# First pair's second and third unit two and three blocks sooner in the bias, values parts one a block from block 31; last block's products ahead of the scores

## The chip, the cores and the metric

The kernel runs on one core of a Trainium2 chip. The metric is the device time of one execution in microseconds (us). The core has five engines with an instruction queue each, taken in order: TensorE (PE in the profile; PEld is its weight load), VectorE (DVE), ScalarE (ACT), GpSimd (POOL) and SyncE (SP, which only issues transfers here). They wait for each other through semaphores.

## What is computed

Attention with a learned position bias over 4 batches, 8 heads, 576 positions and 64 columns a head, and then a feed-forward layer with a convolution of width 3 and a gate. Cut from the reference:

```python
rel = (pos[:, None] - pos[None, :])
x = (np.log1p(np.abs(rel)) / np.log1p(np.maximum(pos[:, None], 1.0)))[..., None]
bias = np.maximum(x @ w1 + b1, 0.0) @ w2
scores = scale * np.matmul(q, k.transpose(0, 1, 3, 2)) + bias.transpose(2, 0, 1)[None]
attn = softmax(scores)
x = heads_side_by_side(np.matmul(attn, v))
h = np.maximum(x @ w_in, 0.0)
out = (h * sigmoid(conv(h))) @ w_out
```

## The kernel before

The bias comes first. It depends on the row i and on the distance of i and j alone, and it is computed in 36 blocks of 16 rows (`NBLK`). `bias_hidden(blk)` makes the hidden layer of one block, four tiles `y` of four rows each: three on DVE (line 329) and one on ACT (line 325), in blocks 14, 15, 30 and 31 all four on DVE. `bias_mm(blk)` multiplies them with the second layer's weights on PE (operands `y,pars`) into one of two PSUM pairs, and `bias_out(blk)` copies the sums out on ACT (line 372; one call for two blocks from block 4 to block 31, else one a block) and lets SP store them in DRAM as `bias_d`. Four `y` buffers rotate. The DRAM copy is what turns distances into rows: `load_bias(0, t)` reads the bias tile `bt` of 128 query rows (64 for t = 0) back. SP issues stores and loads in the order of the code, and a load waits at the head of SP's queue for the stores that it reads.

The attention goes by pairs of heads, pair (n) by n = 0 to 15, and each pair by five units t of query rows. A unit is: `scores` of head 0 (PE, `qk`), `reduce` of head 0 (DVE, line 480, which adds `bt`, takes the maximum and writes `sp`), the same for head 1, `expo` of each head (ACT, line 494), transposes (PE, line 111), and copies of the transposed tile to `ptx` or `pty` (one on ACT, line 152, two on DVE, line 155). In the first units all scores go through one PSUM pair, so `scores` of head 1 waits until `reduce` of head 0 has read it. After unit 2 of a pair the products with the values can be made: `pv_parts` gives five parts of two matmuls (PE, `ptx,vt`), and with the fifth part a copy of the sum to `x` on ACT (line 152, 128x320).

Four units of the first pair, (0,0) to (0,3), are woven into the 36 blocks. `starts` holds the block at which each begins, and `unit_steps` is a generator that gives one step a block: scores and reduce of head 0, of head 1, then expo of head 0, of head 1, then the transposes with their copies. In one block the code emits first `bias_hidden` of the next block, then a step of PE, then the block's own products, then `bias_out` of the block before. The value parts wait in `fill`, and the loop takes some from block `starts[-1]` on; the rest is emitted after the loop. The second half of unit (0,3), unit (0,4) and all units of the later pairs follow after the loop, two units of scores ahead of the transposes: unit (1,0), (1,1), (1,2), (0,4), (1,3) and so on. Unit (0,4) needs the bias tile of the last 128 rows, which the blocks up to 35 make (`load_bias(0, 4, (96,))`: rows 0 to 95 in one load for each head, the rest in another).

Of the kernel before, what the change touches and what calls it, by code (L numbers as in the profile page):

```python
# [18 lines left out]
def attention_ffn_kernel(  # L19
# [75 lines left out]
    def use(ins, ap):  # L95
        name, engine = ap.tensor.name, ins.ins.engine
        before = {}
        for k in spans[name]:
            if latest[k] and latest[k][1] != name and latest[k][2] != engine:
                before[latest[k][0].ins.name] = True  # L100
            latest[k] = (ins, name, engine)
        for other in before:
            tc.add_manual_dep(ins.ins, other, mybir.DependencyInfo(
                mybir.DependencyClass.Sync, mybir.DependencyReason.DATA))
        return ins

    def mm(o, *args, **kw):
        return use(nc.tensor.matmul(o, *args, **kw), o)  # L108
# [89 lines left out]
    with tc.manual_schedule():  # L198
# [53 lines left out]
        def load_bias(p, t, cuts=()):  # L252
            queue = nc.sync
            bt = bias_p.tile([P, 2, S], F32, name="bt") if t else bias0_p.tile([P, 1, S], F32, name="bt0")
            for a, e in zip((0,) + cuts, cuts + (P,)):
                for h in range(2):
                    c = (2 * p + h) * BW
                    if t:
                        i0 = TL + (t - 1) * P
                        queue.dma_start(bt[a:e, h], bias_rows[i0 + a:i0 + e, c:c + S])  # L260
                    else:
                        queue.dma_start(bt[TL * h:TL * h + TL, 0, :], bias_rows[0:TL, c:c + S])
            biast[p, t] = bt
# [44 lines left out]
        def reach(blk):  # L308
            i0 = 16 * (blk - blk % 2)
            return S - i0, i0 + 31  # L310


        def relu_from(blk):
            return 4 if blk // 2 % 8 == 7 else 3

        def bias_hidden(blk):
            full = max(reach(blk)[0], reach(blk)[1] + 1)
            ys = []
            for j in range(4):
                ig = 4 * blk + j  # L320
                n = max(S - 4 * ig, 4 * ig + 4) if 4 <= blk < 32 else full
                row = ybuf[blk % 4][:, j] if j < 3 else y3[:, blk % 4]
                y = row[:, 0:n]
                if j >= relu_from(blk):
                    nc.scalar.activation(  # L325
                        y, dist[:, 0:n], AF.Relu, bias=pars[:, 1:2], scale=inv[:, ig:ig + 1]
                    )
                else:
                    nc.vector.tensor_scalar(  # L329
                        y, dist[:, 0:n], inv[:, ig:ig + 1], nb1, op0=ALU.mult, op1=ALU.max  # L330
                    )
                ys.append(row[:, 0:full])
            return ys
# [3 lines left out]
        def bias_mm(blk, ys):  # L337
            n = ys[0].shape[1]
            if n > 512 or blk % 2 == 0:
                bias_ps[blk] = wide()  # L340
            else:
                bias_ps[blk] = bias_ps[blk - 1]
            ps = bias_ps[blk]
            for a in range(0, n, 512):
                for j in range(4):
                    mm(
                        ps[32 * j:32 * j + 32, a // 512 if n > 512 else blk % 2, 0:min(n - a, 512)],
                        w2b,
                        ys[j][:, a:min(n, a + 512)],
                        start=True,  # L350
                        stop=True,
                    )

        def bias_out(blk):
            nf, nr = reach(blk)
            n = max(nf, nr + 1)
            ps = bias_ps.pop(blk)
            st = sts[blk // 2 % 5].rearrange("p (b n) -> p b n", b=2)
            if n > 512:
                o, i = st[:, blk % 2:blk % 2 + 1], ps.rearrange("p (b a) x -> p b (a x)", b=1)  # L360
            else:
                o, i = st, ps
            fwd = nf > nr


            if n > 512 or blk % 2:
                k = relu_from(blk) - 3
                for oo, ii in (
                    (slice(nr, nr + nf), slice(0, nf)) if fwd else (slice(0, nr + 1), slice(nr, None, -1)),
                    (slice(0, nr), slice(nr, 0, -1)) if fwd else (slice(nr + 1, nr + nf), slice(1, nf)),  # L370
                ):
                    use(nc.scalar.activation(  # L372
                        o[:, :, oo], i[:, :, ii], AF.Identity, bias=kv[:, k:k + 1], scale=inv_scale
                    ), ps)
            if blk == NBLK - 2:
                at = 64 + blk * P * BW - nr
                nc.sync.dma_start(
                    bias_d[at:at + P * BW].rearrange("(p c) -> p c", c=BW)[:, 0:nr + nf], st[:, 0, 0:nr + nf]
                )
            if blk % 2 == 0:  # L380
                return
            at = 64 + (blk - 1) * P * BW - nr
            dst = bias_d[at:at + 2 * P * BW].rearrange("(b p c) -> p b c", b=2, c=BW)
            if blk == NBLK - 1:
                nc.sync.dma_start(dst[:, 1, 0:nr + nf], st[:, 1, 0:nr + nf])
                return
            nc.sync.dma_start(dst[:, :, 0:nr + nf], st[:, :, 0:nr + nf])
# [32 lines left out]
        def turned_sp(n, t):  # L420
            spt[n, t] = (sps[1][spt[n, t][1]], None)
# [53 lines left out]
        def reduce(n, t, h):  # L475
            bt = biast[seq[n][0], t]
            i = pair.pop((n, t, h))
            ps = pairs[i]
            done(i)
            use(nc.vector.tensor_tensor_reduce(  # L480
                out=halves(spt[n, t][0][:, h]),
                in0=ps[:, :, 0:HS],
                in1=halves(bt[:, h]),
                op0=ALU.add,
                op1=ALU.min,
                scale=-scale,
                scalar=3.0e38,
                accum_out=nms[n, t][:, h:h + 1],
            ), ps)

        def expo(n, t, h):
            sp, nm = spt[n, t][0], nms[n, t]
            col = 4 * h + t - 1 if t else 8
            exps[n, t, h] = nc.scalar.activation(  # L494
                sp[:, h], sp[:, h], AF.Exp, bias=nm[:, h:h + 1], scale=-1.0,
                accum_out=sms[n][:, col:col + 1],
            )
# [242 lines left out]
        flat = [(n, t) for n in range(1, NSEQ) for t in units]  # L740
# [3 lines left out]
        def heads(t):  # L744
            return (0, 1) if t else (0,)

        fill = deque()

        def unit_steps(n, t):

            for h in heads(t):
                scores(n, t, h)
                reduce(n, t, h)
                yield h < heads(t)[-1]
            for h in heads(t):
                expo(n, t, h)
                if h == heads(t)[-1]:
                    turned_sp(n, t)
                yield h == heads(t)[-1]
            side = None  # L760
            if t:
                side = pairs[2][:, :, HS:HS + TL]
                side_transposes(side, n, t)
            place_all(transposes(n, t), n, t, side)
            del spt[n, t]
            if ends_group(n, t):
                fill.extend(pv_parts(n, t > 2))
            yield None

        hidden = bias_hidden(0)  # L770
# [4 lines left out]
        load_v(1)  # L775
        last = None
        unit, on_pe = None, None
        starts = [13, 21, 29, 34]
        for i in range(NBLK):
            nxt = bias_hidden(i + 1) if i + 1 < NBLK else None  # L780
            if i in starts:
                unit, on_pe = unit_steps(*first[starts.index(i)]), True
            stepped = bool(on_pe)
            if on_pe:
                on_pe = next(unit)
            bias_mm(i, hidden)
            if last:
                bias_out(*last)
            last = (i,)
            hidden = nxt  # L790
            if i == 5 or i > 6 and i % 8 == 6:
                load_bias(0, i // 8)
            if on_pe is False and not stepped:
                on_pe = next(unit)
            for _ in range(max(0, i - starts[-1] + 1)):
                fill.popleft()()
        bias_out(*last)
        load_bias(0, 4, (96,))
        scores(*flat[1], 0)
        reduce(*flat[1], 0)  # L800
        for h in heads(flat[0][1]):
            expo(*flat[0], h)
        turned_sp(*flat[0])
        while fill:
            fill.popleft()()
# [7 lines left out]
        for u, (n, t) in enumerate(flat[:7]):  # L813
# [18 lines left out]
            i = turned_in.pop((n, t))  # L832
# [457 lines left out]
```

## Time and profile before

| | us |
|---|---|
| median of 3 runs | 473.8 (473.74 to 475.83) |
| the profiled execution | 473.89 |
| its span, first to last instruction | 472.1 |
| PE busy | 456.6 (97%) |
| DVE busy | 361.0 (76%) |
| ACT busy | 308.1 (65%) |

The profiled execution is one of those that the median stands for; 1.8 us of it lie outside its span. Busy shares are means over the whole kernel: DVE and ACT carry the bias in the first 60 us, PE the rest. The granted clock of PE was 0.996 of full speed in the mean.

### The profile page before, as it was taken

How to read it: one execution, taken by the hardware profiler on the slowest of the kernel's cores; microseconds unless marked ns; L12 is line 12 of the kernel's file. 1: busy time of each engine (PE TensorE's matmuls, PEld its weight loads, DVE VectorE, ACT ScalarE, POOL GpSimd, SP SyncE). 2: the span in 40 equal slices, each digit the busy share in tenths (PEclk: the TensorE clock that was granted, in tenths of full speed). 3: DMA queues.
4: the chain of work that ended last, by engine and by line, in shares of the span. 5: the costliest groups of instructions: out<-in, count | busy, mean ns of one | idle time of the engine just before them, and what ended most of it. 6: DMA issues, size and time to landing. Idle time of an engine off the chain costs nothing.

```text
span 472.1 us, 10937 instructions
## 1 busy us (share of the span) xinstructions
PE 456.6 (97%) x4095; PEld 342.2 (72%) x4095; DVE 361.0 (76%) x833; ACT 308.1 (65%) x754; POOL 155.6 (33%) x182
## 2 busy tenths in 40 slices
PE   5987899999999999999999999999999999999996
PEld 3333356777787768877786678988888888888886
DVE  6999967899999799988998631991698159936971
ACT  6989876898888898888888622961453136414530
POOL 1000000583777437781775535006002400060000
PEclk9989999999999999999999999999999999999999
DMA  6798748699678987688673310002000200020002
GB/s 155 205 340 308 265 159 183 173 277 235 174 174 198 280 198 185 148 290 204 160 168 96 116 51 1 2 1 89 1 0 1 96 16 0 1 91 0 1 11 100
DMA packets 34536, 60.81 MB, mean 129 GB/s; under 512 B 6300, under 2 KB 15028, under 8 KB 34484
## 3 DMA queue, kind: packets, MB, share of 16 engines
q1 hardware_dynamic: 34100, 59.78, 44.9%
q8 instruction: 32, 0.52, 0.5%
q10 hardware_dynamic: 384, 0.35, 0.2%
q14 instruction: 20, 0.16, 0.1%
HBM read 44.12 MB, written 15.98 MB: 127 GB/s over the span
## 4 chain that ended last, share of the span: by engine, by line
PE 88%; DMA 4%; DVE 3%; ACT 3%; SPq 1%; issue 1%; DVEq 0%
PE pair L108 38%; PE bank L108 38%; PE bank L111 10%; DMA bias_d<-st 2%; DVE y L329 1%; DMA qk<-in_qk_dram 1%; PE pair L111 1%; ACT st L372 1%; DVE sp L480 1%; ACT y L325 1%; DMA pars<-in_par_dram 1%; DMA bt<-bias_d 1%; ACT sp L494 1%; DVE ptx L155 0%; ACT tl L372 0%
## 5 line engine op out<-in xcount | busy, mean ns | idle before, releaser
L494 ACT ACTIVATE sp<-sp,nm 128x576 f32<-128x576 f32 x144 | 110.8, 771 | 2.3 <-DVE nm L480 1.3
L480 DVE CUSTOM_DVE_ANT_0 sp<-pair,bt 128x576 f32<-128x576 f32 x144 | 105.4, 751 | 8.3 <-PE pair L108 4.8
L108 PE MATMUL pair<-xs,wi 128*128 128x512 f32 x384 | 88.6, 390 | 0.0
L108 PE MATMUL bank<-wo,g 128*128 128x512 f32 x384 | 87.7, 389 | 0.0
L108 PEld LDWEIGHTS pair<-xs,wi 128*128 128x128 f32 x384 | 71.8, 188 | 15.7 <-issue 0.9
L108 PEld LDWEIGHTS bank<-wo,g 128*128 128x128 f32 x384 | 72.0, 188 | 14.9
L111 PE MATMUL bank<-identr,sr 64*128 64x64 f32 x1184 | 63.1, 246 | 1.9 <-ACT sp L494 1.7
L111 PEld LDWEIGHTS bank<-identr,sr 64*128 64x128 f32 x1184 | 56.0, 136 | 11.1 <-ACT ptx L152 5.4
L1075 DVE SCALAR_TENSOR_TENSOR cv<-h,cw,cv 128x575 f32<-128x575 f32 x64 | 52.4, 818 | 12.6 <-ACT cv L1070 10.6
L694 ACT ACTIVATE h<-pair 128x512 f32<-128x512 f32 x32 | 19.1, 598 | 60.4 <-PE pair L108 55.4
L329 DVE TENSOR_SCALAR y<-tl,inv,nb 128x576 f32<-128x576 f32 (+33 forms) x112 | 47.6, 508 | 0.0
L108 PE MATMUL bank<-ptx,vt 128*64 128x320 f32 x320 | 47.0, 438 | 0.0
L194 POOL TENSOR_SCALAR xs<-x 128x512 fp32r<-128x512 f32 (+1 forms) x16 | 11.2, 702 | 105.4 <-DVE gt L1095 105.3
L233 POOL TENSOR_SCALAR hi<-qk 128x640 fp32r<-128x640 f32 (+1 forms) x27 | 19.2, 711 | 80.9 <-DMA qk<-in_qk_dram 79.4
L108 PE MATMUL pair<-y,pars 128*32 128x512 f32 (+8 forms) x352 | 42.7, 511 | 1.7 <-DVE y L329 0.7
L108 PE MATMUL pair<-qk 64*128 64x288 f32 (+1 forms) x280 | 41.2, 433 | 2.0 <-DVE nm L480 1.8
L236 POOL TENSOR_TENSOR ql<-qk,hi 128x640 fp32r<-128x640 f32 (+1 forms) x27 | 40.9, 1513 | 2.3
L152 ACT ACTIVATE ptx<-bank 128x256 f32<-128x256 f32 (+1 forms) x92 | 33.5, 398 | 12.1 <-PE bank L111 11.3
L108 PE MATMUL bank<-pty,vt 128*64 128x256 f32 x320 | 38.1, 384 | 0.0
L1081 ACT ACTIVATE cv<-cv 128x576 f32<-128x576 f32 x32 | 21.9, 684 | 21.9 <-DVE cv L1075 21.8
L1082 DVE SCALAR_TENSOR_TENSOR cv<-cv,h 128x576 f32<-128x576 f32 x32 | 24.1, 753 | 14.0 <-ACT cv L1081 14.0
L108 PEld LDWEIGHTS pair<-y,pars 128*32 128x32 f32 x352 | 15.4, 114 | 26.3 <-DVE y L329 10.7
(89 smaller groups left out, 704.2 us busy)
## 6 DMA issues: line engine op xcount, KB each, us to landing
qk<-in_qk_dram SPq DMA_DIRECT2D x32, 320.0 KB
bt<-bias_d SPq DMA_DIRECT2D x30, 288.0 KB
bias_d<-st SPq DMA_DIRECT2D x13, 607.0 KB
qk<-in_qk_dram SPq DMA_DIRECT2D x32, 144.0 KB
rb<-r_d SPq DMA_DIRECT2D x32, 144.0 KB
vt<-in_v_dram SPq DMA_DIRECT2D x16, 256.0 KB
raw_w<-in_moe_w_in_dram SPq DMA_DIRECT2D x16, 256.0 KB
out_dram<-o SPq DMA_DIRECT2D x16, 256.0 KB
```

The costliest lines, as they stand in the source:

```text
L108: return use(nc.tensor.matmul(o, *args, **kw), o)
L111: return use(nc.tensor.transpose(o, *args), o)
L152: return noted(nc.scalar.activation(o, i, AF.Copy), i)
L233: first = nc.gpsimd.tensor_scalar(hi[:, cs], x[:, cs], 1.0, 0.0, op0=ALU.mult, op1=ALU.add)
L236: nc.gpsimd.tensor_sub(lo[:, cs], x[:, cs], hi[:, cs].bitcast(F32))
L329: nc.vector.tensor_scalar(y, dist[:, 0:n], inv[:, ig:ig + 1], nb1, op0=ALU.mult, op1=ALU.max)
L480: use(nc.vector.tensor_tensor_reduce(out=halves(spt[n, t][0][:, h]), in0=ps[:, :, 0:HS], in1=halves(bt[:, h]), op0=ALU.add, op1=ALU.min, s ...
L494: exps[n, t, h] = nc.scalar.activation(sp[:, h], sp[:, h], AF.Exp, bias=nm[:, h:h + 1], scale=-1.0, accum_out=sms[n][:, col:col + 1],)
L694: use(nc.scalar.activation(h[:, 0:NM], ps[:, 0], AF.Relu), ps)
L1075: nc.vector.scalar_tensor_tensor(out=cv[:, o:o + S - 1], in0=h[:, i:i + S - 1], scalar=cw[:, f, kk:kk + 1], in1=cv[:, o:o + S - 1], op0=AL ...
L1081: nc.scalar.activation(cv, cv, AF.Tanh, scale=0.5)
L1082: nc.vector.scalar_tensor_tensor(out=cv, in0=cv, scalar=1.0, in1=h, op0=ALU.add, op1=ALU.mult)
```

## The change

Three things are moved, and no instruction is added or removed. In `starts`, unit (0,1) begins at block 19 where it was 21, and unit (0,2) at block 26 where it was 29. The value parts of unit (0,2)'s group are taken one a block from block 31, where they were taken one in block 34, two in block 35 and two behind the loop. In the last block the products of the bias come before the scores of head 1 of unit (0,3), and behind the loop `expo` of that unit's head 0 is emitted before `bias_out(35)`, not behind the scores and the reduce of unit (1,0).

```diff
-        starts = [13, 21, 29, 34]
+        starts = [13, 19, 26, 34]
         for i in range(NBLK):
             nxt = bias_hidden(i + 1) if i + 1 < NBLK else None
             if i in starts:
                 unit, on_pe = unit_steps(*first[starts.index(i)]), True
             stepped = bool(on_pe)
+            if nxt is None:
+                bias_mm(i, hidden)
             if on_pe:
                 on_pe = next(unit)
-            bias_mm(i, hidden)
+            if nxt:
+                bias_mm(i, hidden)
             if last:
                 bias_out(*last)
...
-            for _ in range(max(0, i - starts[-1] + 1)):
+            if i >= 31 and fill:
                 fill.popleft()()
+        expo(*flat[0], 0)
         bias_out(*last)
         load_bias(0, 4, (96,))
         scores(*flat[1], 0)
         reduce(*flat[1], 0)
-        for h in heads(flat[0][1]):
-            expo(*flat[0], h)
+        expo(*flat[0], 1)
         turned_sp(*flat[0])
```

DVE's queue around blocks 20 to 22 (`y_123` to `y_125` are the tiles of blocks 20 to 22, `sp_60` is what the reduces of unit (0,1) write):

```order
 L329 TENSOR_SCALAR y_123<-tl,inv,nb_133 128x332 [waits PE_49]
-L329 TENSOR_SCALAR y_124<-tl,inv,nb_133 128x340 [waits PE_49]
-L329 TENSOR_SCALAR y_124<-tl,inv,nb_133 128x344 [waits PE_49]
-L329 TENSOR_SCALAR y_124<-tl,inv,nb_133 128x348 [waits PE_49]
-L329 TENSOR_SCALAR y_125<-tl,inv,nb_133 128x356 [waits PE_49]
-L329 TENSOR_SCALAR y_125<-tl,inv,nb_133 128x360 [waits PE_49]
-L329 TENSOR_SCALAR y_125<-tl,inv,nb_133 128x364 [waits PE_49]
 L480 ISA sp_60,nm<-pair,bt 128x576 [waits DMAHW1_49,PE_49]
 L480 ISA nm 128x1
+L329 TENSOR_SCALAR y_124<-tl,inv,nb_133 128x340 [waits DVE_49]
+L329 TENSOR_SCALAR y_124<-tl,inv,nb_133 128x344 [waits DVE_49]
+L329 TENSOR_SCALAR y_124<-tl,inv,nb_133 128x348 [waits DVE_49]
```

The reduce of head 0, which waits for a load of `bt`, stood behind the tiles of block 22 and stands behind those of block 20.

PE's queue of the change from the value part of block 34 on (`y_126` is block 35, `qk_55` unit (0,3), `qk_56` unit (1,0)):

```order
L108 MATMUL bank<-ptx,vt_112 64x320 x2
L108 MATMUL pair<-y_126,pars 32x512 [waits DVE_49,Activation_49]
L108 MATMUL pair<-y_126,pars 32x512 [waits DVE_49] x2
L108 MATMUL pair<-y_128,pars 32x512
L108 MATMUL pair<-y_126,pars 32x64 x3
L108 MATMUL pair<-y_128,pars 32x64
L108 MATMUL pair<-qk_55 128x288 [waits DVE_49]
L108 MATMUL pair<-qk_55 128x288
L108 MATMUL bank<-ptx,vt_112 64x320 [waits DMAHW7_49,Pool_49]
L108 MATMUL bank<-ptx,vt_112 64x320 [waits DMAHW0_49]
L108 MATMUL pair<-qk_56 64x288 [waits DMAHW2_49,DMAHW1_49,DVE_49]
```

Before, the scores of unit (0,3), head 1, stood ahead of block 35's products; the first part stood in block 34, two stood behind block 35's products, and two behind unit (1,0).

ACT's queue at the end of the loop (`st_131` is written by `bias_out(34)` and then by `bias_out(35)`, `sp_59` is unit (0,3), `sp_60` unit (1,0), `x_127` the copy that goes with the fifth value part):

```order
 L372 ACTIVATE st_131<-pair,kv 128x31
-L372 ACTIVATE st_131<-pair,kv 128x576 [waits PE_49]
+L152 ACTIVATE x_127<-bank 128x320 [waits PE_49]
+L494 ACTIVATE sp_59,sm<-sp_59,nm 128x576 [waits DVE_49]
+L372 ACTIVATE st_131<-pair,kv 128x576
 L372 ACTIVATE st_131<-pair,kv 128x31
-L494 ACTIVATE sp_59,sm<-sp_59,nm 128x576 [waits DVE_49] x2
-L152 ACTIVATE x_127<-bank 128x320 [waits PE_49]
+L494 ACTIVATE sp_59,sm<-sp_59,nm 128x576 [waits DVE_49]
 L494 ACTIVATE sp_60,sm<-sp_60,nm 128x576 [waits DVE_49]
```

`bias_out(35)` stood directly behind `bias_out(34)`; now the copy of the fifth part's sum and one exponential stand between the two.

## Rows read from the trace of the kernel before

**Rows 1.** Windows; behind the colon the length, then each engine's busy time.

```profile
60.00:80.00 20.00, 19.66 (x214) 11.71 (x214) 13.60 (x41) 14.83 (x40) 0.00 (x0) 1.00 0.72 189
80.00:472.00 392.00, 388.22 (x3471) 311.01 (x3467) 293.05 (x654) 241.34 (x626) 153.91 (x168) 1.00 0.40 107
```

**Rows 2.** Chain of work that ended last, in order of time: start, us, what.

```profile
22.44 2.95 DMA bt<-bias_d
...
57.23 0.80 DVE ptx L155 x2
...
74.09 0.83 PE bank L111 x16
```

**Rows 3.** DVE timeline, several stretches: start, us, instructions, idle before and its releaser.

```profile
33.65 1.20 DVE L329 TENSOR_SCALAR y<-tl,inv,nb 128x340 f32<-128x340 f32 x3
...
42.73 0.29 DVE L155 COPY ptx<-pair 128x128 f32<-128x128 f32 x1 [0.49 <-PE pair L111]
43.43 0.69 DVE L155 COPY ptx<-bank 128x512 f32<-128x512 f32 x1 [0.41 <-PE bank L111]
...
45.29 0.94 DVE L329 TENSOR_SCALAR y<-tl,inv,nb 128x452 f32<-128x452 f32 x2
...
54.24 1.05 DVE L329 TENSOR_SCALAR y<-tl,inv,nb 128x544 f32<-128x544 f32 x2
...
70.23 0.76 DVE L480 CUSTOM_DVE_ANT_0 sp<-pair,bt 128x576 f32<-128x576 f32 x1
```

**Rows 4.** SP timeline, issues of loads and of the last store.

```profile
32.11 0.81 SPq L260 DMA_DIRECT2D bt<-bias_d  x2
...
42.61 0.81 SPq L260 DMA_DIRECT2D bt<-bias_d  x2
...
63.10 0.33 SPq L385 DMA_DIRECT2D bias_d<-st  x1
...
65.75 0.77 SPq L260 DMA_DIRECT2D bt<-bias_d  x2
```

**Rows 5.** PE timeline, blocks 33 to 35 and after.

```profile
56.47 1.13 PE L108 MATMUL pair<-y,pars 128*32 128x512 f32 x16
57.52 0.76 PE L108 MATMUL pair<-qk 64*128 64x288 f32 x4
58.21 1.18 PE L108 MATMUL pair<-y,pars 128*32 128x512 f32 x16
59.32 0.76 PE L108 MATMUL bank<-ptx,vt 128*64 128x320 f32 x4
...
60.91 1.18 PE L108 MATMUL pair<-y,pars 128*32 128x512 f32 x16
62.02 1.30 PE L108 MATMUL bank<-ptx,vt 128*64 128x320 f32 x8
63.24 0.72 PE L108 MATMUL pair<-qk 64*64 64x288 f32 x8
63.89 1.30 PE L108 MATMUL bank<-ptx,vt 128*64 128x320 f32 x8
```

**Rows 6.** ACT timeline behind the last block.

```profile
62.15 0.92 ACT L372 ACTIVATE st<-pair,kv 128x576 f32<-128x576 f32 x2 [1.78 <-PE pair L108]
62.96 0.77 ACT L494 ACTIVATE sp<-sp,nm 128x576 f32<-128x576 f32 x1
...
65.26 0.44 ACT L152 ACTIVATE x<-bank 128x320 f32<-128x320 f32 x1 [0.68 <-PE bank L108]
65.59 0.77 ACT L494 ACTIVATE sp<-sp,nm 128x576 f32<-128x576 f32 x1
```

**Rows 7.** Windows: length, busy PE, PEld, DVE, ACT, POOL; then PE's granted clock.

```profile
25.20:26.90 1.70, 0.36 (x2) 0.00 (x0) 1.34 (x4) 1.49 (x3) 0.00 (x0) 1.00 1.05 409
...
28.60:32.20 3.60, 3.60 (x24) 1.63 (x24) 3.55 (x11) 2.91 (x6) 0.00 (x0) 0.53 1.02 392
...
40.50:42.20 1.70, 0.25 (x2) 0.00 (x0) 1.70 (x5) 1.70 (x4) 0.00 (x0) 1.00 0.56 220
```

## The prediction

> **What bounds the kernel now.** I read the windows by stage first. From 80 us to the end PE is busy 388.22 of 392 us, and in the stage behind the bias, 60 to 80 us, 19.66 of 20 [rows 1]. So whatever the change does to the first 80 us reaches the end of the kernel as the shift of the point from which PE never waits again. The chain of waits says where that point is: up to 74 us the chain changes between PE and DVE, and at 74.09 us, with the transposes of unit (0,4), it goes over to PE for good [rows 2]. These transposes wait for the end of a dense run of DVE work which begins at 70.23 us with the first reduce of unit (0,4) [rows 3]. The question is therefore when that reduce can start. It needs three things: DVE's own work before it, the scores on PE, and the last bias tile, which comes through ACT (`bias_out(35)`), a store, and a load. Before, the last of the loads of that tile was issued by 65.75 us [rows 4] and the reduce shows no wait for it: the tile was early, by an amount to be worked out.
>
> **The units moved up.** These steps keep their count; only the waits change. DVE is nearly gapless in the bias, so I count its idle time. Unit (0,1)'s first reduce now stands behind block 20's tiles, which end where block 21's begin, 33.65 us [rows 3]. The load of its bias tile is issued at 32.11 us [rows 4], and its place in SP's queue and the store that it waits for are not touched. The one load that the chain shows took 2.95 us from issue to landing [rows 2], so the tile lands at 35.06 and DVE stands 1.41 us. The bounds are 0 (the tile is there) and 1.41, since the load of 2.95 us had a second one beside it as this has; I take 1.41. Behind the waiting reduce stand the tiles of blocks 21 and on, so PE and ACT come later too. In return DVE no longer stands 0.49 + 0.41 us for the transposes of that unit [rows 3]: its exponentials now lie two blocks earlier, and DVE has other blocks' tiles ahead of the copies. Unit (0,2)'s first reduce is ready behind block 27's tiles, 45.29 us before [rows 3], some 45.8 now; its load is issued at 42.61 [rows 4] and lands at 45.56 by the same price. That is a margin of a quarter microsecond, so I cost it at nothing, and what it costs without the margin is a rival below. Its two copies, 0.80 us [rows 2], now come ahead of block 32's tiles. Those were ready at 54.24 us [rows 3]; now at 54.24 + 0.80 + 1.41 - 0.90 = 55.55.
>
> **The value parts.** Two parts take 1.22 us (from 62.02 to 63.24), so one takes 0.61; the products of one block take 1.05 us (blocks 33) or 1.11 (34, 35), and a head's scores 0.69 [rows 5]. A block from 32 on costs DVE three tiles at half of 1.05 us, some 1.5 us [rows 3]; PE now has 1.05 + 0.61 = 1.66 a block, and 0.69 more in block 34. So in these four blocks PE takes over as the bound, and the parts are not hidden. From 55.55: 1.05 + 0.61 (block 32 and a part), 1.05 + 0.61 (33), 0.69 + 1.11 + 0.61 (34), 1.11 (35) make 6.84, and block 35's products end at 62.39, against 62.02 before. Then come head 1's scores, to 63.08, and the fifth part.
>
> **The order behind the last block.** This is where the sum is decided. ACT takes its queue in order, and the copy of the fifth part's sum and one exponential now stand ahead of `bias_out(35)`. The copy started 1.37 us after the last two parts did (63.89 to 65.26) [rows 5, 6], so 0.76 after a part's start: 63.84. The copy takes 0.33 (65.26 to 65.59), the exponential 0.77, so `bias_out(35)` begins at 64.94; it takes 0.81 (62.15 to 62.96) [rows 6], and the store follows 0.14 later, at 65.89. Before it was issued at 63.10 [rows 4]: 2.79 us later, although the products it copies are only 0.37 later. What the moved exponential gains, its own early start, nobody waits for, since head 1's exponential stands behind `bias_out(35)` again.
>
> The last loads of the tile waited for the store, 63.10 to 65.75, so 2.65 us from issue to landing [rows 4]; they are now issued at 68.54. How long they take no row shows. The bounds: not over 4.48, as the reduce at 70.23 did not wait for them; from below their issue alone, 0.77 for both [rows 4]. The nearest rows are the 2.65 of a store and the 2.95 of a load; I take 2.8. Then the tile lands at 71.34, the reduce that began at 70.23 waits until then, and unit (0,4)'s transposes are 1.11 us late. The shorter work on PE (two parts fewer between the last block and unit (1,1), 1.22 us) is spent in this wait.
>
> The Trainium skill, page "DMA: Bandwidth & Descriptors", section "Anatomy of one DMA", gives a fixed cost of about 2.0 us, mostly the receipt of the write, plus the bytes at 436 GB/s. For the store of 304 KB that makes an estimate of 2.7, which agrees with the 2.65 here; for a load of 72 KB at most it makes 2.2, by which the sum would be 0.5 us, not 1.1.
>
> The sum is made on the profiled execution, 473.89 us, which is 0.1 above the median: 473.89 + 1.1 = 475.0. As PE has no idle time behind 74 us in which to win it back [rows 1], all of it stays.
>
> **The rivals.** A change of under 0.5%, that is 2.4 us (below 471.4 or above 476.2), is about what a measurement of this kernel can't tell from none.
>
> First, the tile lands in time. If the last loads take 1.7 us or less, or the copy's wait is shorter, the reduce is not held up, and what remains is PE: unit (1,0)'s scores begin at 64.1 (they wait for head 1's reduce) against 63.24 [rows 5], with 1.22 us of parts less behind them, so 0.4 earlier: 473.5. For it speaks that the bounds of the load are wide; against it that both rows near it are over 2.6.
>
> Second, the change does all that it could: the loads of unit (0,1) have landed, DVE stays ahead, and all four parts behind the last tiles, 2.4 us, go into PE's idle time: 471.5. Against it speaks that PE has 1.66 us or more to do in blocks of 1.5.
>
> Third, on the slow side: PE's clock. Where PE was busy only 0.36 of 1.70 us (25.20 to 26.90), its clock stood at half soon after (a mean of 0.53, the level of 1.2 GHz, from 28.60 to 32.20); in the equally empty stretch from 40.50 to 42.20 (0.25 of 1.70) it stayed full [rows 7]. The change moves PE's gaps: one now lies behind unit (0,1)'s waiting reduce, and one near 50 us, ahead of unit (0,2)'s transposes. If the clock falls behind the latter, a halved stretch as long as that one, 3.6 us at the most, covers blocks 31 to 33, in which PE is now the bound, and costs half of itself, 1.7 us or so: 475.0 + 1.7 = 476.7. It decides if the clock is at half anywhere between 52 and 62 us. The Trainium skill, "TensorE: Matmul & The Clock Gate", Part 1, says that an array that has idled runs at 1.2 GHz until it has been busy for a while; the trace agrees with 0.53 behind the first gap, and the window at 40.50 shows that not every gap does it.
>
> Fourth, unit (0,2)'s bias tile is late. The load at 42.61 waits behind slow stores; if the stall in unit (0,1) passes 1 us on to the store it waits for, DVE stands for 0.8 us more at block 27, and all behind it: 475.8, and as much as 476.5 if the second head waits too.
>
> **The numbers.** The forecast, ACT's queue holding up the last tile, has 0.52, and its own range is 474.3 to 475.8. The tile in time: 0.28. All hidden: 0.04. The clock: 0.08. Unit (0,2)'s tile late: 0.08. Faster by over 0.5% has the 0.04 of the second; slower over 476.2 has the clock and half of the last rival's upper end, 0.11; the rest, 0.85, is within 0.5%. The range for 8 in 10 leaves out the second rival and most of the third: 472.9 to 476.4; its upper part also takes in a load of 4.48 us, which would make the delay 2.79.
>
> **What would show it.** In the profile after, a DVE wait of about 1.4 us for `bt` near 33.7 us; PE with no gap from block 32 to unit (1,0)'s scores; ACT idle behind `bias_out(34)` until the 128x320 copy at about 63.8; the last store issued at about 65.9; a DVE wait for `bt` ahead of unit (0,4)'s reduce, which starts at about 71.3; and the transposes of unit (0,4), from which on PE stays busy, at 75.2 where they were at 74.09. The forecast is wrong if the last loads land within 1.7 us of their issue, if DVE reaches block 32 much sooner than 55.5, or if PE's clock falls in the tail of the bias.

## The result, and the profile after

The changed kernel takes 476.5 us (median of 10 executions, 474.65 to 478.74), the kernel before beside it on the same chip 473.8 (10 executions, 472.44 to 475.83). The ratio is 1.0056, with a 95% interval of 1.0037 to 1.0076: slower by 2.7 us. The forecast was 475.0, its range ended at 476.4.

The profiled execution of the changed kernel took 475.04 us, which is the forecast to a few hundredths. That is partly luck: only one of the ten executions was shorter. It is read first, by the forecast's steps; then the question is what the other executions do that this one does not. Its page begins:

```profile
span 473.3 us, 10941 instructions
...
PE 456.5 (96%) x4095; PEld 342.5 (72%) x4095; DVE 361.2 (76%) x833; ACT 308.1 (65%) x754; POOL 155.7 (33%) x182
```

No engine does more work than before; the span is longer by 1.2 us of waiting. DVE's timeline of the changed kernel (start, us, instructions, idle before and its releaser) holds most of the steps:

```profile
35.26 0.76 DVE L480 CUSTOM_DVE_ANT_0 sp<-pair,bt 128x576 f32<-128x576 f32 x1 [1.58 <-DMA bt<-bias_d]
...
37.19 0.76 DVE L480 CUSTOM_DVE_ANT_0 sp<-pair,bt 128x576 f32<-128x576 f32 x1
...
41.34 0.29 DVE L155 COPY ptx<-pair 128x128 f32<-128x128 f32 x1
41.55 0.68 DVE L155 COPY ptx<-bank 128x512 f32<-128x512 f32 x1
...
45.84 0.76 DVE L480 CUSTOM_DVE_ANT_0 sp<-pair,bt 128x576 f32<-128x576 f32 x1
...
54.17 5.86 DVE L329 TENSOR_SCALAR y<-tl,inv,nb 128x544 f32<-128x544 f32 x12
60.01 0.76 DVE L480 CUSTOM_DVE_ANT_0 sp<-pair,bt 128x576 f32<-128x576 f32 x1
...
71.53 0.76 DVE L480 CUSTOM_DVE_ANT_0 sp<-pair,bt 128x576 f32<-128x576 f32 x1 [0.52 <-PE bank L111]
```

Unit (0,1)'s first reduce stands 1.58 us for its bias tile. The two copies of that unit, which stood 0.49 and 0.41 us for PE before [rows 3], don't stand at all. Unit (0,2)'s reduce at 45.84 waits for nothing. The twelve tiles of the last four blocks begin at 54.17, three to a block, so block 32 is ready at 54.17 + 3 x 0.49 = 55.6. The row at 60.01 is unit (0,3)'s first reduce. The last row is unit (0,4)'s reduce, at 70.23 before [rows 3].

PE's timeline of the changed kernel from block 32 on:

```profile
55.18 1.66 PE L108 MATMUL pair<-y,pars 128*32 128x512 f32 x16
56.77 0.76 PE L108 MATMUL bank<-ptx,vt 128*64 128x320 f32 x4
...
61.69 1.18 PE L108 MATMUL pair<-y,pars 128*32 128x512 f32 x16
62.80 0.76 PE L108 MATMUL pair<-qk 64*128 64x288 f32 x4
63.48 0.76 PE L108 MATMUL bank<-ptx,vt 128*64 128x320 f32 x4
64.42 0.81 PE L108 MATMUL pair<-qk 64*64 64x288 f32 x8 [0.18 <-DVE nm L480]
```

There is no wait in these rows until unit (1,0)'s scores: products, a value part, products again. Behind the last block, ACT's timeline and then SP's:

```profile
64.32 0.44 ACT L152 ACTIVATE x<-bank 128x320 f32<-128x320 f32 x1 [2.26 <-PE bank L108]
64.65 0.77 ACT L494 ACTIVATE sp<-sp,nm 128x576 f32<-128x576 f32 x1
...
65.41 0.91 ACT L372 ACTIVATE st<-pair,kv 128x576 f32<-128x576 f32 x2
```

```profile
66.34 0.33 SPq L385 DMA_DIRECT2D bias_d<-st  x1
66.78 2.59 SPq L260 DMA_DIRECT2D bt<-bias_d  x4
```

`bias_out(35)` stands on ACT behind the copy to `x` and an exponential, as forecast; the last store is issued at 66.34 where it was 63.10 [rows 4]. What unit (0,4)'s reduce waits for is the second load of head 0: by the landing records in the trace it was issued at 68.60 and its last part landed at 71.37, 0.16 us before the reduce began. The row names PE as the releaser, because PE's transposes, from 70.50 on, also ended just before; but in the kernel before the reduce began (70.23) while the same transposes were still running (69.68 to 70.52). From there the delay goes on as forecast: in the chain of work of the changed kernel (start, us, what) the transposes from which PE stays busy come at 75.39, before at 74.09 [rows 2].

```profile
75.39 0.84 PE bank L111 x16
```

So in this execution the sum held: the span is 1.2 us longer, for 1.1. The median is 1.4 us above this execution, and that is what the experiments are about. Four of the ten executions have a mean granted clock of PE of .993 or less (477.49 to 478.74 us); the other six lie between 474.65 and 476.48.

### The profile page after: what moved, and what is told of

Its sections match the earlier page's. It is cut to its first block, busy times and chain, and to the rows that moved or that the text cites. A ratio compares the mean times of both kernels' runs of the same rounds, so it can differ in the third digit from the quotient of the medians.

```text
span 473.3 us, 10941 instructions
## 1 busy us (share of the span) xinstructions
PE 456.5 (96%) x4095; PEld 342.5 (72%) x4095; DVE 361.2 (76%) x833; ACT 308.1 (65%) x754; POOL 155.7 (33%) x182
## 4 chain that ended last, share of the span: by engine, by line
PE 89%; ACT 3%; DVE 3%; DMA 3%; issue 1%; DVEq 0%; SPq 0%
PE pair L108 40%; PE bank L108 38%; PE bank L111 10%; DVE y L329 2%; ACT st L372 2%; DMA bias_d<-tl 1%; PE pair L111 1%; ACT y L325 1%; DVE sp L480 1%; DMA pars<-in_par_dram 1%; DMA bt<-bias_d 1%; ACT sp L494 0%; DVE ptx L155 0%; ACT tl L372 0%; ACT x L152 0%
## 5 line engine op out<-in xcount | busy, mean ns | idle before, releaser
L236 POOL TENSOR_TENSOR ql<-qk,hi 128x640 fp32r<-128x640 f32 (+1 forms) x27 | 40.9, 1514 | 2.3
L645 POOL TENSOR_TENSOR x<-x,rb 128x576 f32<-128x576 f32 x16 | 23.1, 1445 | 32.8 <-DMA rb<-r_d 30.5
```

Of the source, the lines that this page charges most:

```text
L236: nc.gpsimd.tensor_sub(lo[:, cs], x[:, cs], hi[:, cs].bitcast(F32))
L645: return nc.gpsimd.tensor_mul(xb[b][:, p], xb[b][:, p], rbs.pop(n))
```

## The experiments

All times are medians; e5 and e11 also hold the three products told of there; before's is that of its executions beside the same kernels: 474.4 (34 executions, e1 to e4), 474.3 (35, e5 to e8), 474.2 (28, e9 to e12). "Low" counts the executions with a mean granted clock of .993 or less; before has 8 in these 97. A mean does not say where in the execution the clock fell.

| run | starts | parts early | last block new | us (range, n) | ratio to before, 95% | low |
|---|---|---|---|---|---|---|
| e1_unit1_back | 13, 21, 26, 34 | yes | yes | 475.59 (474.35 to 476.65, 12) | 1.0021 (1.0008 to 1.0035) | 1 |
| e2_units_only | 13, 19, 26, 34 | no | no | 476.15 (474.53 to 480.30, 12) | 1.0042 (1.0022 to 1.0062) | 6 |
| e3_last_only | 13, 21, 29, 34 | no | yes | 473.58 (473.06 to 474.67, 12) | 0.9984 (0.9973 to 0.9995) | 0 |
| e4_fifth_back | 13, 19, 26, 34 | four of five | yes | 477.02 (474.86 to 478.01, 11) | 1.0044 (1.0030 to 1.0059) | 6 |
| e5_hold_clock | 13, 19, 26, 34 | yes | yes | 476.31 (475.41 to 477.26, 12) | 1.0040 (1.0027 to 1.0053) | 0 |
| e6_no_parts | 13, 19, 26, 34 | no | yes | 476.16 (474.89 to 479.53, 12) | 1.0046 (1.0025 to 1.0067) | 5 |
| e7_parts_last | 13, 21, 29, 34 | three of five | yes | 474.84 (474.40 to 476.22, 12) | 1.0016 (1.0003 to 1.0029) | 1 |
| e8_unit2_only | 13, 21, 26, 34 | no | no | 474.29 (473.40 to 476.15, 12) | 1.0004 (0.9990 to 1.0018) | 1 |
| e9_unit1_only | 13, 19, 29, 34 | no | no | 475.89 (474.71 to 478.24, 11) | 1.0043 (1.0026 to 1.0060) | 4 |
| e10_unit1_at20 | 13, 20, 29, 34 | no | no | 474.40 (473.56 to 475.87, 12) | 1.0002 (0.9991 to 1.0014) | 1 |
| e11_unit1_hold | 13, 19, 29, 34 | no | no | 475.32 (474.63 to 476.36, 10) | 1.0030 (1.0019 to 1.0042) | 0 |
| e12_changed_again | 13, 19, 26, 34 | yes | yes | 476.55 (476.23 to 480.60, 6) | 1.0064 (1.0037 to 1.0091) | 4 |

The theory after the result was that unit (0,1)'s earlier start costs more than the forecast gave it, by its stall and by what the stall does to PE's clock. The rivals were the value parts and the order behind the last block (which the forecast held to be the cost), and unit (0,2).

**e1_unit1_back.** The changed kernel with unit (0,1) at its old block.

```diff
-        starts = [13, 19, 26, 34]
+        starts = [13, 21, 26, 34]
```

> The changed kernel with unit (0,1) back at block 21, all else as changed. Then DVE doesn't stand for the first bias tile of that unit (1.58 us in the changed kernel) and PE has no empty stretch there. Theory of the clock: of the 2.7 us, 1.2 are the last bias tile's delay behind ACT's queue, and the rest comes from executions in which PE's clock falls a second time after the empty stretch near 34 us; so the median falls by 1.5 or more, to 474.4 to 475.0, and hardly any execution has a mean clock of 0.993 or less. Rival, the queue alone (clock scatter has nothing to do with the change): only the stall's net 0.5 us goes, median 475.8 to 476.2, and the spread of the executions stays as in the changed kernel (474.7 to 478.7).

475.59, 0.9 us below the changed kernel's 476.5 and 1.5 nearer to before (+1.2 for +2.7), with one low execution in 12. Unit (0,1) is the larger part, or half if the changed kernel's second measurement (+2.3, e12) is taken. The median lies between the two expectations.

**e2_units_only.** The kernel before with the two starts alone.

```diff
-        starts = [13, 21, 29, 34]
+        starts = [13, 19, 26, 34]
```

> The kernel before with units (0,1) and (0,2) started at blocks 19 and 26; the value parts and the end of the loop as before. The stall at block 20 is there, ACT's queue at the end is as before. Theory of the clock: 1 to 2 us slower than before in the median (475 to 475.8), with executions of a lower mean clock among them. Rival, the queue alone: 0.5 us slower at most (474.3), spread as before; no wait for the last bias tile in either.

476.15: the starts alone bring +1.8 of the +2.7, where the forecast's terms had given them about 0.5 (1.41 of stall less 0.90). That agrees with the theory of the clock (1 to 2 us), not with its rival. The profiled execution is the slowest of the 12, 480.30 us, and shows why. DVE's timeline, then the windows (length; busy PE, PEld, DVE, ACT, POOL; granted clock; DMA share; GB/s):

```profile
38.05 0.76 DVE L480 CUSTOM_DVE_ANT_0 sp<-pair,bt 128x576 f32<-128x576 f32 x1 [4.28 <-DMA bt<-bias_d]
...
45.44 0.29 DVE L155 COPY ptx<-pair 128x128 f32<-128x128 f32 x1 [0.94 <-PE pair L111]
46.49 0.69 DVE L155 COPY ptx<-bank 128x512 f32<-128x512 f32 x1 [0.75 <-PE bank L111]
```

```profile
36.30:38.00 1.70, 0.00 (x0) 0.00 (x0) 0.00 (x0) 0.00 (x0) 0.00 (x0) 0.99 1.04 403
38.00:42.00 4.00, 3.12 (x20) 1.20 (x22) 3.62 (x10) 1.47 (x3) 0.00 (x0) 0.50 0.60 235
42.00:46.00 4.00, 2.90 (x32) 1.33 (x24) 2.79 (x8) 2.79 (x5) 0.00 (x0) 0.50 0.22 87
46.00:51.60 5.60, 5.60 (x36) 1.83 (x34) 4.38 (x10) 4.75 (x7) 0.00 (x0) 0.50 0.73 250
```

The same load that cost 1.58 us in the changed kernel's profile costs 4.28 here. All four compute engines stand still from 36.30 to 38.00, while the DMA engines are full (share 1.04). Then PE has its clock at half, the level of 1.2 GHz, for 13.6 us, and the copies stand for its transposes again, 0.94 and 0.75 us.

The landing records of this execution show one more thing. A load of `bt` lands in 16 parts, each recorded. Fifteen parts of the load that DVE waits for had landed by 35.22 us; the sixteenth landed at 37.92, and the reduce began at 38.05. Meanwhile one packet of 16 KB was under way in the instruction queue, from 34.04 to 36.29 us. The view of the DMA queues from 34 to 36.3 us has it as one packet that takes 6.1%, a sixteenth, of the time of the 16 DMA engines, so one engine for nearly the whole stretch:

```profile
q8 instruction: 1, 0.02, 6.1%
```

In e9's profile it is the same: fifteen parts by 35.67, the last at 36.91, the packet from 33.89 to 35.27. In the kernel before the packet comes at 36.01, when both heads' loads have landed (34.90 and 35.92). Of the 168 loads of `bt` issued in the first 75 us of the fourteen profiles, 31 had a last part that came over 0.8 us behind the other fifteen. In all 31 such a packet was under way before the last part landed; of the 112 loads without one, none had a last part so late.

**e3_last_only.** The kernel before with the last block and the exponential alone.

```diff
+            if nxt is None:
+                bias_mm(i, hidden)
             if on_pe:
                 on_pe = next(unit)
-            bias_mm(i, hidden)
+            if nxt:
+                bias_mm(i, hidden)
...
+        expo(*flat[0], 0)
         bias_out(*last)
```

> The kernel before with only the last block changed: its products ahead of the scores, and head 0's exponential ahead of its copy. Both theories: no stall, no empty stretch, no fifth part ahead of the copy; the last store about 1 us sooner than before, but nobody waits for it; 473.3 to 473.9.

473.58, 0.8 us faster than before, and the fastest of all, as expected. Here the copy to `x` is not yet on ACT when `bias_out(35)` comes, so the cost of that order is absent. SP's timeline has the last store at 61.92 (63.10 before [rows 4]), and the chain has the transposes at 73.59 (74.09 before [rows 2]):

```profile
61.92 0.33 SPq L385 DMA_DIRECT2D bias_d<-st  x1
```

```profile
73.59 0.84 PE bank L111 x16
```

The sooner store itself gains nothing, for unit (0,4)'s reduce did not wait for its tile before either. Of the 0.50 us at the transposes, 0.26 is there at unit (0,3)'s first reduce (59.13, before 59.39 as shown under e4), ahead of any changed code; 0.24 comes behind it, where the scores that wait for the reduce no longer stand ahead of the last products. What makes the rest of the 0.8 is not shown.

**e4_fifth_back.** The changed kernel with the fifth part, and so its copy to `x`, behind the loop again.

```diff
-            if i >= 31 and fill:
+            if 31 <= i < 35 and fill:
```

> The changed kernel with the fifth value part (and its copy on ACT) behind the loop, so that no copy stands ahead of the last block's copy. The last store goes out some 2.4 us sooner (63.9 against 66.3 us) and the wait for the last bias tile goes. Queue theory: 0.6 to 1.2 us faster than the changed kernel. Clock theory: the same, and the spread to long executions of low clock stays, since the empty stretch near 34 us stays: median 475.2 to 475.9. If the whole loss were the queue's, the median would go to 474.

477.02 against 476.5, ratio 1.0044 to before against 1.0056: no gain shows in the median, where both theories had expected 0.6 us or more. In its profile SP's timeline has the store 2 us sooner than in the changed kernel, and DVE's has the reduce of unit (0,4) at 71.47 without a wait. The first row of the second view is unit (0,3)'s first reduce; the last view has that of the kernel before:

```profile
64.37 0.33 SPq L385 DMA_DIRECT2D bias_d<-st  x1
```

```profile
60.51 0.76 DVE L480 CUSTOM_DVE_ANT_0 sp<-pair,bt 128x576 f32<-128x576 f32 x1
...
71.47 0.76 DVE L480 CUSTOM_DVE_ANT_0 sp<-pair,bt 128x576 f32<-128x576 f32 x1
```

```profile
59.39 0.77 DVE L480 CUSTOM_DVE_ANT_0 sp<-pair,bt 128x576 f32<-128x576 f32 x1
```

The tile is in time now: the load that the reduce needs landed at 70.49. That the reduce comes at 71.47, as in the changed kernel's profile (71.53), does not mean that nothing was won, for this execution was 0.50 us behind that one already at unit (0,3)'s first reduce (60.51 for 60.01), by a longer stall in block 20. From that reduce to unit (0,4)'s it takes 10.84 us before, 11.52 in the changed kernel, and 10.96 here. So in the end of the bias the fifth part and its copy are worth 0.56 us in the profiles, which is less than the median of 11 executions can tell (the interval is 0.7 us to either side).

**e5_hold_clock.** The changed kernel with three products that nobody reads, in PE's queue ahead of the scores that wait behind unit (0,1)'s reduce.

```diff
+            if i == 20:
+                for _ in range(3):
+                    mm(banks[6][:, 0:512], ident, dist[:, 0:512], start=True, stop=True)
             if on_pe:
                 on_pe = next(unit)
```

> The changed kernel with three matmuls added on PE (128x512, to a bank that nobody reads then) directly ahead of the scores that wait behind unit (0,1)'s stalled reduce; they fill the empty stretch near 34 us and compute nothing that is used. Theory of the clock: executions with a mean clock of 0.993 or less vanish, and the median falls from 2.7 us above the kernel before to 1.0 to 1.7. Rival, that the late landing of the bias tile alone makes the long executions: the clock rows change but the median stays at 2.3 to 2.9 above.

No execution of 12 is low, and the longest ends at 477.26 (478.74 without the three products). But the median is 476.31, lower by 0.2 only, +2.0 to before, between the two expectations. The fallen clock makes the long executions; most of the median's distance to before stays without it.

**e6_no_parts.** The changed kernel with the old rule for the value parts.

```diff
-            if i >= 31 and fill:
+            for _ in range(max(0, i - starts[-1] + 1)):
```

> The changed kernel with the value parts taken by the old rule (one in block 34, two in 35, two behind the loop). If the parts ahead of the last blocks cost (PE bound there, as the sum has it), this is 0.6 to 1.2 us faster than the changed kernel: 1.0 to 1.9 above the kernel before (units alone stand at 1.8 above, the last block alone at 0.8 below). If they cost nothing, it stays at 2.4 to 2.9 above.

476.16, +1.8 to before, as in e2: no better than the units alone. The gain that e3 has by itself does not show here; the two intervals overlap, and the run settles no more than that the parts are not the main cost. In its profile PE's clock is at half behind the unit's gap too (0.50 from 37.6 to 40.9 us), and yet the copies at 42.03 and 42.23 wait for nothing: a fallen clock there does not always cost DVE time.

**e7_parts_last.** The changed kernel with the old starts.

```diff
-        starts = [13, 19, 26, 34]
+        starts = [13, 21, 29, 34]
```

> The changed kernel with both units back at blocks 21 and 29: the parts one a block (from block 33, when the first exists) and the last block changed. No stall at block 20. Two parts stay behind the loop, so the copy stays behind the last block's copy. Clock theory: 0.8 below to 0.2 above the kernel before, no execution of low clock. If the units were not what costs, it is over 1 us above.

474.84, +0.5, between the two expectations. From e3 the run differs only in that two of the three early parts stand one block sooner; beside e3's -0.8 that costs 1.3 us. The copy to `x` is not ahead of `bias_out(35)` here, so the run does not test the forecast's order on ACT.

**e8_unit2_only.** The kernel before with unit (0,2) three blocks sooner.

```diff
-        starts = [13, 21, 29, 34]
+        starts = [13, 21, 26, 34]
```

> The kernel before with unit (0,2) alone moved, from block 29 to 26. Its bias tile has a margin of a quarter us by the sum, so a small stall in some executions: 0 to 0.6 above the kernel before, and no execution of low clock by the clock theory, whose empty stretch is unit (0,1)'s. If unit (0,2)'s tile comes late as a rule: 1 to 2 us above.

474.29, no change shown (ratio 1.0004, 0.9990 to 1.0018). Its profiled execution does show a DVE wait for the tile, of 0.80 us, and yet takes 474.64:

```profile
46.34 0.76 DVE L480 CUSTOM_DVE_ANT_0 sp<-pair,bt 128x576 f32<-128x576 f32 x1 [0.80 <-DMA bt<-bias_d]
```

So the cost of e2 should be unit (0,1)'s. The next three take that unit alone.

**e9_unit1_only.** The kernel before with unit (0,1) in block 19.

```diff
-        starts = [13, 21, 29, 34]
+        starts = [13, 19, 29, 34]
```

> The kernel before with one number changed: unit (0,1) starts in block 19 instead of 21; the other starts, the value parts and the last block stay. Theory 'unit (0,1) alone is the cost' (its reduce stands for its bias tile, by a time that differs from execution to execution): about +1.8 us, as when both units moved (476.15), so 475.6 to 476.4, and some executions with a mean clock of .993 or less, as 6 of 12 had there. Rival 'it takes both units moved': 474.3 to 474.9, and hardly an execution with a low clock.

475.89, +1.7, and four low executions in 11: all of e2's cost. DVE's timeline of its profiled execution, which is the median one (475.89 us, granted clock 0.995):

```profile
37.04 0.76 DVE L480 CUSTOM_DVE_ANT_0 sp<-pair,bt 128x576 f32<-128x576 f32 x1 [2.85 <-DMA bt<-bias_d]
...
42.98 0.29 DVE L155 COPY ptx<-pair 128x128 f32<-128x128 f32 x1
43.31 0.69 DVE L155 COPY ptx<-bank 128x512 f32<-128x512 f32 x1
...
72.55 0.76 DVE L480 CUSTOM_DVE_ANT_0 sp<-pair,bt 128x576 f32<-128x576 f32 x1
```

The tile costs 2.85 us, the copies give 0.90 back, which leaves 1.95. Unit (0,4)'s reduce is 2.32 late (70.23 before [rows 3]); 0.53 of that was there ahead of the stall, since block 20's tiles end at 34.18 (33.65 before [rows 3]), so 1.8 comes from the unit. The span is 2.0 longer, and PE's clock was whole behind the stall. DVE is the pace of the bias: nearly all that it stands for and does not get back at the copies arrives at the end.

**e10_unit1_at20.** The kernel before with unit (0,1) in block 20.

```diff
-        starts = [13, 21, 29, 34]
+        starts = [13, 20, 29, 34]
```

> The kernel before with unit (0,1) started in block 20, halfway. Its first reduce then stands one block, some 1.2 us, later than in the changed kernel, at 34.8 to 35, while its tile's first half landed at 34.9 to 35.7 in most of the profiled executions and its second half at 35.9 to 38.1. Theory 'the stall is the price': a stall of 0.3 to 1 us, so +0.2 to +0.9: 474.5 to 475.3. Theory 'it is PE's clock': the empty stretch of PE is shorter by the stall that is gone, the clock holds, and the time is that of before, 474.3, with the low-clock executions as rare as in before.

474.40, ratio 1.0002: nothing. In its profile DVE stands 0.29 us for the tile.

```profile
35.89 0.76 DVE L480 CUSTOM_DVE_ANT_0 sp<-pair,bt 128x576 f32<-128x576 f32 x1 [0.29 <-DMA bt<-bias_d]
```

This execution, 475.87 us, is the slowest of the 12 and the only low one; its clock was at half from 28.60 to 34.30 (0.50), ahead of the unit. The cost begins between the two blocks: in block 20 the reduce comes at about the landing, in block 19 well ahead of it. As stall and gap go together here, the run does not tell one from the other.

**e11_unit1_hold.** e9 with e5's three products in block 20.

```diff
-        starts = [13, 21, 29, 34]
+        starts = [13, 19, 29, 34]
...
+            if i == 20:
+                for _ in range(3):
+                    mm(banks[6][:, 0:512], ident, dist[:, 0:512], start=True, stop=True)
```

> The kernel before with unit (0,1) started in block 19 and three products of 128x512, which nobody reads, put into PE's queue in block 20, where PE otherwise stands empty behind the waiting reduce. Beside the same start without them: theory 'PE's clock' has the executions with a low clock disappear and the median fall to within 0.6 of before, 474.3 to 474.9; theory 'the stall itself' has the executions with a low clock disappear too, since these products keep PE busy, but the median stay at over 475.3.

475.32, no low execution in 10. Of e9's +1.7, 1.1 stays without any low execution and 0.6 goes (the intervals, 1.0026 to 1.0060 and 1.0019 to 1.0042, overlap, so the split is rough). Its windows show PE busy, and its clock whole, where the changed kernel's PE is empty:

```profile
33.70:35.40 1.70, 1.70 (x11) 0.70 (x8) 0.61 (x2) 1.70 (x4) 0.00 (x0) 1.00 0.88 225
36.00:38.00 2.00, 2.00 (x11) 0.65 (x13) 1.46 (x5) 2.00 (x5) 0.00 (x0) 1.00 1.04 397
```

The three products are not free, though: head 1's reduce in this profile, the slowest of the 10, waited 1.62 us for its scores. So the split between stall and clock is not shown: some of the 1.1 may be the products' own cost.

**e12_changed_again.** The changed kernel once more.

> The changed kernel once more, beside the others on one chip. If its scatter is its own and not that of one occasion: a median of 476 to 477, and about 4 in 10 executions with a mean clock of .993 or less and 477.4 or more.

476.55, four low in 6, two of these near the median (476.48 and 476.56). Its profiled execution, 476.56 us, is a typical one, and can be laid beside the first profile (475.04 us) as the same program. DVE's timeline:

```profile
35.15 0.76 DVE L480 CUSTOM_DVE_ANT_0 sp<-pair,bt 128x576 f32<-128x576 f32 x1 [1.22 <-DMA bt<-bias_d]
...
37.19 0.76 DVE L480 CUSTOM_DVE_ANT_0 sp<-pair,bt 128x576 f32<-128x576 f32 x1 [0.17 <-DMA bt<-bias_d]
...
42.13 0.29 DVE L155 COPY ptx<-pair 128x128 f32<-128x128 f32 x1 [0.70 <-PE pair L111]
42.84 0.69 DVE L155 COPY ptx<-bank 128x512 f32<-128x512 f32 x1 [0.41 <-PE bank L111]
...
47.33 0.76 DVE L480 CUSTOM_DVE_ANT_0 sp<-pair,bt 128x576 f32<-128x576 f32 x1
...
72.97 0.76 DVE L480 CUSTOM_DVE_ANT_0 sp<-pair,bt 128x576 f32<-128x576 f32 x1 [0.45 <-PE bank L111]
```

Head 1's reduce begins at 37.19 in both. Unit (0,2)'s begins at 47.33 here and at 45.84 there, 1.49 later, and unit (0,4)'s at 72.97 against 71.53, 1.44 later; the whole execution is 1.5 longer. So all of the difference arises between 37.19 and 47.33, and the copies hold 1.11 of it: they stand for PE's transposes again. The stall itself is shorter here (1.39 us, 1.58 there). The windows of the first profile of the changed kernel, and then of this one:

```profile
33.70:35.40 1.70, 0.00 (x0) 0.00 (x0) 0.14 (x1) 1.70 (x4) 0.00 (x0) 1.00 0.95 295
...
37.00:39.00 2.00, 1.68 (x19) 0.62 (x12) 1.95 (x6) 1.26 (x2) 0.00 (x0) 1.00 1.05 410
39.00:41.00 2.00, 1.45 (x19) 0.61 (x16) 2.00 (x7) 2.00 (x5) 0.00 (x0) 1.00 0.59 229
```

```profile
33.70:35.40 1.70, 0.24 (x4) 0.00 (x0) 0.48 (x2) 1.70 (x4) 0.00 (x0) 1.00 1.02 379
...
37.00:39.00 2.00, 2.00 (x16) 0.72 (x18) 1.83 (x6) 0.44 (x1) 0.00 (x0) 0.50 1.05 412
39.00:41.00 2.00, 1.32 (x12) 0.29 (x6) 2.00 (x7) 1.39 (x3) 0.00 (x0) 0.81 0.35 137
```

PE is as good as empty behind the waiting reduce in both, 0.00 and 0.24 of 1.70 us; in the second its clock is at half from 37.00 to 39.00 (0.50), and once more from 43.2 to 46.5 (0.50); in the first it is not. In turn the second kept its clock from 28.60 to 32.20 (1.00), where the first had 0.61.

## Why the prediction was wrong, by its steps

**Unit (0,1)'s stall** is the step that failed. It was priced as 1.41 us less the 0.90 that the copies no longer stand, so 0.51, from one load of one execution, and the 1.41 was taken for the upper bound. Neither half of it is a fixed number. The stall, summed over both heads, was 1.58 (after), 4.28 (e2), 2.08 (e4), 2.15 (e5), 2.00 (e6), 2.85 (e9), 1.27 (e11) and 1.39 (e12) in the eight profiled executions with the unit in block 19: a median of 2.04, with 1.41 near the low end. And the 0.90 can come back where PE's clock falls behind the stall (1.11 in e12, 1.69 in e2; not in e6). The forecast of 0.51 for this unit measured 1.7 alone (e9), and one block later next to nothing (e10). That the unit's early start makes this cost is shown; its split into stall and clock is not (e11). It is the same mechanism with the wrong size, and the missing 1.2 is most of the 1.5 by which the median passed the forecast.

**PE's clock**, the third rival at 0.08, was a mechanism that did occur, at another place. It was looked for near 50 us, ahead of unit (0,2)'s transposes, and was to decide only between 52 and 62 us, where PE is the bound. The gap that mattered was the one behind unit (0,1)'s own reduce, which the prediction named and gave no price. The fall came at about 37 us, and it could cost time there too, because the copies on DVE wait for PE's transposes. The Trainium skill, page "TensorE: Matmul & The Clock Gate", Part 1, has an idle array run at 1.2 GHz until it has been busy for a while: e12 agrees (0.50 behind the gap). The first profile, with an emptier gap, stayed at 1.00, so not every such gap does it.

**Unit (0,2)** at no cost agrees with e8 (474.29 alone), whose interval leaves room for 0.9 us at most. Its tile was late with unit (0,1) at its old block (0.80 us in e8's profile, 0.85 in e1's). In the changed kernel's two profiles it was not, for there unit (0,1)'s stall had made DVE late already; so the fourth rival, which had that stall make this one, is not borne out.

**The value parts making PE the bound** was right: block 32 ready at 55.6 for 55.55, its last products ending near 62.8 for 62.39, the fifth part from 63.48 for 63.08, no gap before unit (1,0)'s scores.

**ACT's queue** was right in each instant of the profile (copy 64.32 for 63.84, store 66.34 for 65.89, tile 71.37 for 71.34, PE busy for good from 75.39 for 75.2). Less the 0.51 of the unit, the forecast's 1.11 leaves 0.60 for the end of the bias. From unit (0,3)'s first reduce to unit (0,4)'s the profiles with all five parts early took 11.52 (after), 11.51 (e1) and 11.45 us (e12) for 10.84 before, so 0.6 to 0.7 more. A fourth, e5, took 11.03; there the load that the reduce needs landed 2.23 us after its issue, and not 2.74 to 2.80 as in the other three. The 2.8 that the prediction chose between wide bounds was thus right in three of four. The 2.2 estimated beside it, from a figure that the Trainium skill, page "DMA: Bandwidth & Descriptors", section "Anatomy of one DMA", gives for the path through GpSimd, agrees with e5 alone; these loads are issued by SP. The first rival, the tile in time, promised 473.5; with the tile in time (e4) the end of the bias was no shorter than before (10.96 us for 10.84).

**The sum**, with the unit's measured size in it, adds up: units +1.8 (e2) and the end of the bias 0.6 to 0.7 (profiles) make 2.4 to 2.5; the changed kernel shows +2.7 at first and +2.3 again (e12). What is left open is why unit (0,1)'s tile lands so differently. DMA engines are full while DVE waits (1.04 in e2's window, 1.02 in e12's), and the longest waits are those for one part of 16 beside a packet of the instruction queue. Both are seen, neither is tested: no run took other transfers away or moved that packet.

The best version of these is e3: the last block's new order alone, 473.58 us, ratio 0.9984 (0.9973 to 0.9995), faster than both kernels.

## What to carry to other kernels

Where an edit moves a consumer to within a microsecond or two of a transfer's landing, price the wait over several executions: one load's time from one trace is one draw. Here the wait for it was 1.3 to 4.3 us, and one block of margin was the difference between +1.7 and nothing. A wait on one engine also empties the engine behind it, so allow for what PE does at half clock afterwards, and don't count an idle time as saved on an engine that waits for PE there. When two profiled executions are laid side by side, first see where they were apart ahead of the edit: equal end times of two executions hid 0.56 us here (e4). Of a change in several parts, time each alone: here one part gained 0.8 us, one showed no cost, and the others hid the gain.

## What the runs showed of the hardware that was not expected

The same read of the same tile, in programs that are alike up to there, let its reader go at 35.15 us in one execution (e12) and at 38.05 in another (e2). In the second, one of the load's 16 parts landed 2.70 us behind the others, beside a 16 KB packet of the instruction queue that took 2.25 us; over the first 75 us of the fourteen profiles 31 of 56 loads with such a packet under way had a last part over 0.8 us late, and none of 112 without. PE's clock after a gap is not settled by the gap alone: with PE empty or nearly so for the same stretch behind unit (0,1)'s reduce (0.00 and 0.24 of 1.70 us), one execution of one program ran on at full clock and another at half (the first had been at half earlier, 0.61 from 28.60 to 32.20, the second not, 1.00). And with three products of 128x512 put into that gap no execution of 22 (e5 and e11) had a mean clock of .993 or less, where 29 of 62 had it in the other programs with that gap (after, e2, e4, e6, e9, e12: 4 of 10, 6 of 12, 6 of 11, 5 of 12, 4 of 11 and 4 of 6).
